# Right-hand blocks one per product, and factors, gates and block sums in idle PSUM banks

## The chip, the cores and the metric

The kernel runs on one core of one Trainium2 chip. The metric is device time in microseconds (us) from launch to end. The kernel before takes 1083.06 us, the median of three runs (1082.38 to 1083.61).

## The reference

Three parts follow one another on 4 batches of 448 rows, all in fp32: an attention with a sigmoid in place of the softmax (12 heads of 64), a gated layer, and a product layer.

```python
attn = 1 / (1 + exp(-(scale * q @ k.T - log(S))))      # S = 448
x    = (attn @ v) as 1792 x 768
xn   = x / sqrt(mean(x * x) + 1e-6) * rms_g
x    = (silu(xn @ w_gate) * (xn @ w_val)) @ w_out      # 768 -> 1536 -> 768
out  = ((x @ w1) * (x @ w2)) @ w3 @ w_out2             # 768 -> 1024 -> 1024 -> 768
```

## The kernel before

**Numbers.** The weights come as doubles. VectorE (DVE) turns them into fp32, and every fp32 operand of TensorE (PE) is split into a high and a low part: ScalarE (ACT) copies the high part (L134 for weights, L357 for activations), and the low part is the operand less the high part, on GpSimd (POOL, L137) for weights and on DVE (L362) for activations. A product runs three times (high by high, low by high, high by low), 448 columns at a time; all of them stand at L343. `w3 @ w_out2` is multiplied once, early, into `w3o`, so the last part has one matrix of 1024 x 768.

**Winograd's form.** For batches 2 and 3 of the gated layer, and for all four batches of the product layer and of the last matrix, a 2 x 2 block product is made with seven products in place of eight. This asks for block sums on three sides:

- sums of weight blocks (`winograd_blocks`, DVE L169, L170, L171, L177): `s1`, `s2` and `s2'` stand in a tile `s`, while the difference of a11 and a21 is written over a21 in the loaded tile `wd`. Each block is then split by ACT and POOL. In the first pass over the product layer the sums are also kept in DRAM for the second pass;
- sums of the right-hand operand (`right_blocks`): seven blocks w0 to w6, some of them factors such as b12 - b11, each split by ACT and DVE;
- sums of the seven products (`combine`, L617 to L637): each product ends in a PSUM bank, and DVE adds it to the sums before it (`u`, `v`, `c11`, `c21`).

**Order.** The stages that use this form are, one after the other: twelve gated tiles (`a_winograd`), the plain output of the gated layer, then for batches 0 and 1 eight product tiles (`c_winograd`, called c1 here) and three output steps (`d_winograd`, d1), and the same for batches 2 and 3 (c2, d2). A tile of `a_winograd` or `c_winograd` is seven products of nine matmuls. Two tiles of `c_winograd` make a pair: their four results `ab` are the four blocks from which the seven right-hand blocks of the output step are made, all in one piece after the pair's second tile. In `d_winograd` a product has two halves of six matmuls, and between the first halves and the second ones `y_blocks` makes seven right-hand blocks for the next pass from four tiles `ys` loaded out of DRAM.

**Queues.** Each engine works through its instructions in program order. A scheduler sorts them when the program is built, so the order of the lines is not quite that of the code.

**PSUM.** There are eight banks: three behind `psm()`, one of `ps_av`, and four behind `bank()`, which the seven products of a tile take in turn, so that a bank is needed again four products later. In c1 and c2 and in `a_winograd` the other four are not used. In `d_winograd` products 4 to 6 (of 0 to 6) stand in the three banks of `psm()`.

## Time and profile before

| | |
|---|---|
| median of three runs | 1083.06 us |
| the profiled execution | 1078.52 us |
| its span, first to last instruction | 1076.7 us |
| PE busy | 1055.8 us, 98% |
| DVE busy | 854.2 us, 79% |
| POOL busy | 507.8 us, 47% |
| ACT busy | 404.1 us, 38% |
| stage a_winograd | 508.7 to 664.3 us |
| stage c1 | 752.45 to 862.2 us |
| stage d1 | 862.2 to 918 us |
| stages c2 and d2 | 918 to 1026 us, 1026 to 1076.7 us |

The profile is of one execution, 4.54 us under the median. Of its 1078.52 us, 1.8 lie outside the span. Times of day in the rows count from the start of the span. In a row of a timeline the brackets hold the idle time of that engine just ahead of the row, and what ended it.

### The profile page before, as it was taken

Reading aid. Unit: us, or ns where it says so; the run is one execution under the profiler, and the core shown is the slowest. Engines: PE = TensorE matmul, PEld = TensorE weight load, DVE = VectorE, ACT = ScalarE, POOL = GpSimd, SP = SyncE. Lnnn points to the kernel's source line nnn. Section 1 sums busy time; section 2 is a strip of 40 time slices with the busy share of each in tenths; the row PEclk is TensorE's granted clock in tenths of the full one; section 3 lists DMA queues with packets and bytes.
Section 4 is the critical chain, followed back from the end, with each engine's and each line's share of the span. In section 5 each row is a group of like instructions: output and inputs, shape, how many; then the busy total and the mean of one; then the engine's idle time right before and its main releaser. Section 6 shows DMA issues by size and latency. Waiting matters only on the chain.

```text
span 1076.7 us, 14161 instructions
## 1 busy us (share of the span) xinstructions
PE 1055.8 (98%) x5080; PEld 884.6 (82%) x5080; DVE 854.2 (79%) x1132; ACT 404.1 (38%) x747; POOL 507.8 (47%) x414
## 2 busy tenths in 40 slices
PE   9999999999999999999999999999999989999998
PEld 4338799997766767699899998999988889999997
DVE  5998999999565787679787778676799899677874
ACT  5673311112243442215544444233333454333441
POOL 3646343543333232342655653233656666555572
PEclk9999999999999999999999999999999999999999
DMA  7743555566452567754311113766532245433221
GB/s 258 261 161 121 148 175 174 194 233 207 139 188 99 204 201 271 238 202 126 106 59 59 59 59 105 257 238 224 169 115 98 80 135 152 152 100 106 65 93 69
DMA packets 71350, 164.25 MB, mean 153 GB/s; under 512 B 7024, under 2 KB 45040, under 8 KB 71280
## 3 DMA queue, kind: packets, MB, share of 16 engines
q1 hardware_dynamic: 71280, 163.35, 45.5%
q8 instruction: 40, 0.66, 0.2%
q14 instruction: 30, 0.25, 0.1%
HBM read 119.67 MB, written 43.65 MB: 152 GB/s over the span
## 4 chain that ended last, share of the span: by engine, by line
PE 48%; DVE 7%; issue 2%; POOL 2%; DMA 2%; ACT 1%; SPq 0%; DVEq 0%; ACTq 0%; POOLq 0%
PE w L343 29%; PE psm L343 18%; POOL ws L137 2%; DVE w L362 1%; DMA wd<-in_wo 1%; DMA raw<-in_qkv 1%; DVE ab L655 1%; DVE s L177 0%; DMA wd<-in_w 0%; ACT ws L134 0%; PE av L454 0%; DVE wf L127 0%; DVE c L627 0%; DVE v L637 0%; DVE wf L116 0%
## 5 line engine op out<-in xcount | busy, mean ns | idle before, releaser
L343 PE MATMUL w<-w,ws 128*128 128x448 f32 x2052 | 424.4, 367 | 9.8 <-DVE v L625 9.0
L343 PEld LDWEIGHTS w<-w,ws 128*128 128x128 f32 x2052 | 385.7, 188 | 46.5 <-DVE v L625 11.8
L137 POOL TENSOR_TENSOR ws<-wf,ws 128x768 fp32r<-128x768 f32 (+1 forms) x92 | 175.4, 1911 | 112.3 <-ACT ws L134 95.0
L343 PE MATMUL psm<-hm,ws 128*128 128x448 f32 x864 | 178.0, 367 | 0.0
L343 PEld LDWEIGHTS psm<-hm,ws 128*128 128x128 f32 x864 | 161.9, 188 | 16.8 <-issue 2.4
L137 POOL TENSOR_TENSOR ws<-wd,ws 128x384 fp32r<-128x384 f32 (+1 forms) x128 | 131.3, 1040 | 75.9 <-ACT ws L134 74.3
L137 POOL TENSOR_TENSOR ws<-s,ws 128x384 fp32r<-128x384 f32 (+1 forms) x96 | 101.7, 1067 | 86.1 <-ACT ws L134 68.1
L136 POOL CAST ws<-wf 128x768 fp32r<-128x768 f32 (+1 forms) x52 | 46.4, 893 | 197.1 <-PE psm L343 98.4
L343 PE MATMUL psm<-x,ws 128*128 128x448 f32 x648 | 136.3, 368 | 0.2 <-DVE s L682 0.2
L343 PEld LDWEIGHTS psm<-x,ws 128*128 128x128 f32 x648 | 120.9, 188 | 17.0 <-issue 3.7
L116 DVE TENSOR_SCALAR wf<-mag 128x768 uint32<-128x768 uint32 (+1 forms) x76 | 67.0, 882 | 34.7 <-POOL ws L137 27.2
L124 DVE SCALAR_TENSOR_TENSOR wf<-wd,wf 128x768 uint32<-128x768 uint32 (+1 forms) x76 | 85.8, 1129 | 2.5
L114 DVE TENSOR_SCALAR mag<-wd 128x768 uint32<-128x768 uint32 (+1 forms) x76 | 52.0, 685 | 36.1 <-DMA wd<-in_wo 19.3
L127 DVE SCALAR_TENSOR_TENSOR wf<-wd,wf 128x768 uint32<-128x768 uint32 (+1 forms) x76 | 79.3, 1044 | 1.4
L134 ACT ACTIVATE ws<-wd 128x384 fp32r<-128x384 f32 (+1 forms) x128 | 57.2, 474 | 53.0 <-PE w L343 39.9
L343 PE MATMUL psm<-o,ws 128*128 128x384 f32 x384 | 70.4, 342 | 0.0
L343 PEld LDWEIGHTS psm<-o,ws 128*128 128x128 f32 x384 | 68.1, 190 | 2.7 <-issue 2.5
L115 DVE TENSOR_SCALAR mag<-mag 128x768 f32<-128x768 f32 (+1 forms) x76 | 64.2, 845 | 1.5
L134 ACT ACTIVATE ws<-s 128x384 fp32r<-128x384 f32 (+1 forms) x96 | 44.4, 475 | 49.4 <-DVE s L170 32.6
L454 PE MATMUL av<-a,raw 128*64 128x448 f32 x288 | 59.4, 548 | 0.0
L357 ACT ACTIVATE hm<-s 128x448 fp32r<-128x448 f32 x48 | 27.7, 576 | 71.3 <-DVE s L686 49.2
L169 DVE TENSOR_TENSOR s<-wd 128x384 f32<-128x384 f32 (+1 forms) x32 | 29.9, 934 | 30.6 <-POOL ws L137 28.7
(102 smaller groups left out, 1245.6 us busy)
## 6 DMA issues: line engine op xcount, KB each, us to landing
raw<-in_qkv SPq DMA_DIRECT2D x23, 736.0 KB, 5.1
wd<-in_wo SPq DMA_DIRECT2D x20, 768.0 KB, 5.6
wd<-in_w SPq DMA_DIRECT2D x16, 768.0 KB, 5.1
wd<-in_wg SPq DMA_DIRECT2D x12, 768.0 KB, 4.6
wd<-in_wv SPq DMA_DIRECT2D x12, 768.0 KB, 5.4
wd<-in_w SPq DMA_DIRECT2D x16, 512.0 KB, 4.3
w<-wf SPq DMA_DIRECT2D x16, 384.0 KB, 2.7
wd<-w SPq DMA_DIRECT2D x16, 384.0 KB, 3.7
```

What stands on the lines that cost most here:

```text
L114: nc.vector.tensor_scalar(out=mag.bitcast(U32), in0=hi, scalar1=0x7FFFFFFF, scalar2=None, op0=ALU.bitwise_and)
L115: nc.vector.tensor_scalar(out=mag, in0=mag, scalar1=HI_MIN, scalar2=HI_MAX, op0=ALU.max, op1=ALU.min)
L116: nc.vector.tensor_scalar(out=u, in0=mag.bitcast(U32), scalar1=3, scalar2=0x3FFFFFFF, op0=ALU.logical_shift_left, op1=ALU.bitwise_and,)
L124: nc.vector.scalar_tensor_tensor(out=u, in0=hi, scalar=0xC0000000, in1=u, op0=ALU.bitwise_and, op1=ALU.bitwise_or)
L127: nc.vector.scalar_tensor_tensor(out=u, in0=lo, scalar=29, in1=u, op0=ALU.logical_shift_right, op1=ALU.bitwise_or)
L134: nc.scalar.activation(t[:, 0, :w], f[:, :w], AF.Copy)
L136: nc.gpsimd.tensor_copy(out=t[:, 0, :w], in_=f[:, :w])
L137: nc.gpsimd.tensor_tensor(out=t[:, 1, :w], in0=f[:, :w], in1=t[:, 0, :w], op=ALU.subtract)
L169: nc.vector.tensor_tensor(out=s1, in0=a21, in1=a22, op=ALU.add)
L343: nc.tensor.matmul(ps, w, xt[:, xi, :], start=first and r == 0 and j == 0, stop=last and r == 2 and j == n - 1)
L357: i = nc.scalar.activation(dst[:, 0, :], src, AF.Copy)
L454: nc.tensor.matmul(av[p][d, :], r[:, v + j * D : v + (j + 1) * D], a[:, j, :], start=False, stop=(c == 2))
```

## The change

Three things are done.

First, the weight sum `s2'` is written over the block a12 in `wd` and no longer into `s`.

Second, the right-hand blocks come from a generator, `right_steps`, which gives one block at each `step()`; a step stands after every product in `combine` and after every first half in `d_winograd`. The low split of a block is issued one step later than its high split. The four results of a pair are used as they come, so three of the seven blocks of a pair are made before its second tile ends. In d1 the `ys` blocks are also spread over steps. Outside these stages (`x_blocks`, `y_blocks(0, k)`) the generator runs through at once.

Third, some DVE results go to PSUM: the factors t1 to t4 (`home`), `c11` and `c12` of gated and product tiles, the gate (silu in place, then times the value), and the fourth `ab` tile of each pair.

```diff
                 yield from (a11, s2, a12, a21, a22, s1)
-                nc.vector.tensor_tensor(out=s2, in0=a12, in1=s2, op=ALU.subtract)
+                nc.vector.tensor_tensor(out=a12, in0=a12, in1=s2, op=ALU.subtract)
                 if keep is not None:
-                    nc.sync.dma_start(out=keep[3], in_=s2)
+                    nc.sync.dma_start(out=keep[3], in_=a12)
...
-    def right_blocks(k, b11, b12, b21, b22, down=False):
+    def right_steps(k, b, home=None, down=False, wait=None):
+        def sub(out, in0, in1, op=ALU.subtract):
+            i = nc.vector.tensor_tensor(out=out, in0=in0, in1=in1, op=op)
+            if down or wait is not None:
+                tc.keep_in_program_order(i)
+        late = []
         def put(j, bl, src):
             t = acts["d" if down else "w", j, k] = ab_tile(f"w{j}", 7 * k + j) if down else right_tile(f"w{j}", bl)
-            split2(t, src)
+            nc.scalar.activation(t[:, 0, :], src, AF.Copy)
+            low()
+            late.append((t, src))
+        def low():
+            if late:
+                t, src = late.pop()
+                sub(t[:, 1, :], src, t[:, 0, :])
+        if wait is None:
+            put(0, 0, b[0])
+            yield
+            t1 = home()
+            sub(t1, b[1], b[0])
+            put(5, 1, t1)
+            yield
+            while len(b) < 4:
+                low()
+                yield
+            put(2, 0, b[2])
+            yield
+            t3 = home()
+            sub(t3, b[3], b[1])
+            put(3, 2, t3)
+            yield
+            t2 = home()
+            sub(t2, t3, b[0], ALU.add)
+            put(1, 2, t2)
+            yield
+            t4 = home()
+            sub(t4, b[2], t2)
+            put(4, 2, t4)
+            yield
+            put(6, 1, b[3])
+            yield
+            low()
+            return
...
+    def y_steps(k):
+        y = load_y(1, k)
+        for _ in range(2):
+            yield
+        yield from right_steps(k, y, wait=5 if k == 2 else 0)
+
+    def product_bank():
+        return psm()[:, :S]
...
-        combine(product, done)
+        combine(product, done, product_bank)
...
         for j in range(7):
             part(2 * n, j)
-        if between:
-            between()
+            step()
...
         p2 = product(2)
+        c11 = home() if home else scratch("c11")
         tt(out=c11, in0=p2, in1=u, op=ALU.add)
+        step()
...
         p3 = product(6)
-        tt(out=v, in0=p3, in1=v, op=ALU.add)
-        done(1, v, u)
+        c12 = home() if home else v
+        tt(out=c12, in0=p3, in1=v, op=ALU.add)
+        done(1, c12, u)
+        step()
...
-            s = scratch("s")
-            nc.scalar.activation(s, g, AF.Silu)
-            nc.vector.tensor_tensor(out=s, in0=s, in1=v, op=ALU.mult)
+            nc.scalar.activation(g, g, AF.Silu)
+            nc.vector.tensor_tensor(out=g, in0=g, in1=v, op=ALU.mult)
...
         def done(b, x, y):
-            t = ab[m % 2, b] = held("ab")
-            nc.vector.tensor_tensor(out=t, in0=x, in1=y, op=ALU.mult)
+            tiles.append(ps_av.tile([P, 512], F32, tag="av", bufs=1, name="ab")[:, :S] if len(tiles) == 3 else held("ab"))
+            nc.vector.tensor_tensor(out=tiles[-1], in0=x, in1=y, op=ALU.mult)
         winograd(first, m, done)
-        if m % 2:
-            right_blocks(m // 2, ab[0, 0], ab[0, 1], ab[1, 0], ab[1, 1], True)
+        if m % 2 == 0:
+            todo.append(right_steps(m // 2, tiles, product_bank, True))
...
     for m in range(KF2):
         c_winograd(i_c, m)
+    todo.extend(y_steps(k) for k in range(KD // 2))
     for n in range(KD // 2):
-        d_winograd(0, i_d, n, lambda: y_blocks(1, n))
+        d_winograd(0, i_d, n)
```

The counts of instructions of every engine stay as they were; what changes is where they stand and which tile they write. In the rows that follow, numbers behind a name tell instances apart, and the lines of the changed kernel are its own (L550 is `sub`, L699 the sum `v`, L703 `c11`, L718 `c12`, L738 the product tile, L178 `s2'`).

The first place is the end of a pair in c1, on DVE, in the kernel before:

```order
L655 TENSOR_TENSOR ab_6574<-v_6466,u_6465 128x448
L170 TENSOR_TENSOR s_6621<-s_6621,wd_6529 128x384
L556 TENSOR_TENSOR t1_6576<-ab_6574,t1_6576 128x448
L558 TENSOR_TENSOR ab_6463<-ab_6574,ab_6463 128x448
L560 TENSOR_TENSOR ab_6544<-ab_6544,t1_6576 128x448
L362 TENSOR_TENSOR w1_6588<-t1_6576,w1_6588 128x448
L362 TENSOR_TENSOR w3_6592<-ab_6463,w3_6592 128x448
L362 TENSOR_TENSOR w4_6596<-ab_6544,w4_6596 128x448
L362 TENSOR_TENSOR w6_6599<-ab_6574,w6_6599 128x448
L171 TENSOR_TENSOR wd_6529<-wd_6529 128x384
L625 TENSOR_TENSOR v_6603<-w_6631,u_6602 128x448
```

Seven operations on right-hand blocks stand in one piece (L556 to the last L362) ahead of the sum `v` of the next tile (L625). In the changed kernel the same place reads:

```order
L718 TENSOR_TENSOR psm_6588<-w_6578,v_6473 128x448
L738 TENSOR_TENSOR ab_6590<-psm_6588,u_6472 128x448
L550 TENSOR_TENSOR psm_6622<-ab_6590,ab_6470 128x448
L550 TENSOR_TENSOR w2_6592<-ab_6559,w2_6592 128x448
L699 TENSOR_TENSOR v_6595<-w_6627,u_6594 128x448
L550 TENSOR_TENSOR psm_6638<-psm_6622,ab_6437 128x448
L550 TENSOR_TENSOR w3_6624<-psm_6622,w3_6624 128x448
L178 TENSOR_TENSOR wd_6544<-wd_6544,s_6612 128x384
L703 TENSOR_TENSOR psm_6658<-w_6643,u_6594 128x448
L550 TENSOR_TENSOR psm_6660<-ab_6559,psm_6638 128x448
L550 TENSOR_TENSOR w1_6640<-psm_6638,w1_6640 128x448
```

Ahead of `v` (L699) stand now the product tile, one factor and one low split; the other factors follow between the sums of the next tile, and those named psm are in PSUM.

The second place is the start of d1 on PE: the first half of product 4 of its first step (three runs of two matmuls, psm_7388) and the start of product 5, with what each instruction waits for. Before:

```order
L343 MATMUL psm_7388<-w4_6596,ws_7297 128x448 [waits Activation_49]
L343 MATMUL psm_7388<-w4_6853,ws_7297 128x448
L343 MATMUL psm_7388<-w4_6596,ws_7297 128x448 [waits Pool_49]
L343 MATMUL psm_7388<-w4_6853,ws_7297 128x448
L343 MATMUL psm_7388<-w4_6596,ws_7297 128x448
L343 MATMUL psm_7388<-w4_6853,ws_7297 128x448
L343 MATMUL psm_7389<-w5_6581,ws_7297 128x448 [waits Activation_49]
```

Products 4 and 5 wait for ACT, which makes the high part of a block. In the changed kernel, where psm_7395 and psm_7396 are these products:

```order
L344 MATMUL psm_7395<-w4_6662,ws_7327 128x448 [waits DVE_49,Activation_49]
L344 MATMUL psm_7395<-w4_6924,ws_7327 128x448
L344 MATMUL psm_7395<-w4_6662,ws_7327 128x448 [waits Pool_49]
L344 MATMUL psm_7395<-w4_6924,ws_7327 128x448
L344 MATMUL psm_7395<-w4_6662,ws_7327 128x448
L344 MATMUL psm_7395<-w4_6924,ws_7327 128x448
L344 MATMUL w_7391<-w0_7010,ws_7358 128x448 [waits Activation_49]
L344 MATMUL psm_7396<-w5_6513,ws_7327 128x448 [waits DVE_49]
```

Product 4 now waits for DVE too and product 5 for DVE, and one matmul of product 0's bank (w_7391) has moved ahead of product 5. The rows of DVE at the end of the last pair, before:

```order
L362 TENSOR_TENSOR w2_7366<-ab_7316,w2_7366 128x448 [waits Activation_49]
L655 TENSOR_TENSOR ab_7356<-v_7237,u_7236 128x448 [waits DVE_49]
L177 TENSOR_TENSOR s_7332<-wd_7272,s_7332 128x256 [waits Pool_49]
L556 TENSOR_TENSOR t1_7358<-ab_7356,t1_7358 128x448 [waits DVE_49]
L558 TENSOR_TENSOR ab_7234<-ab_7356,ab_7234 128x448
L560 TENSOR_TENSOR ab_7316<-ab_7316,t1_7358 128x448 [waits DVE_49]
L362 TENSOR_TENSOR w1_7370<-t1_7358,w1_7370 128x448 [waits Activation_49]
L362 TENSOR_TENSOR w3_7374<-ab_7234,w3_7374 128x448 [waits Activation_49]
L362 TENSOR_TENSOR w4_7378<-ab_7316,w4_7378 128x448 [waits Activation_49]
L362 TENSOR_TENSOR w6_7381<-ab_7356,w6_7381 128x448
L169 TENSOR_TENSOR s_7428<-wd_7340 128x256 [waits DMAHW4_49,Pool_49]
```

and in the changed kernel:

```order
L718 TENSOR_TENSOR psm_7385<-w_7375,v_7259 128x448 [waits DVE_49,PE_49]
L178 TENSOR_TENSOR wd_7295<-wd_7295,s_7362 128x256 [waits Pool_49]
L738 TENSOR_TENSOR ab_7387<-psm_7385,u_7258 128x448 [waits DVE_49]
L550 TENSOR_TENSOR psm_7411<-ab_7387,ab_7256 128x448 [waits DVE_49]
L550 TENSOR_TENSOR w2_7389<-ab_7346,w2_7389 128x448
L550 TENSOR_TENSOR psm_7422<-psm_7411,ab_7222 128x448 [waits Activation_49]
L550 TENSOR_TENSOR w3_7413<-psm_7411,w3_7413 128x448
L170 TENSOR_TENSOR s_7450<-wd_7370 128x256 [waits DMAHW5_49,Pool_49]
L550 TENSOR_TENSOR psm_7433<-ab_7346,psm_7422 128x448 [waits Activation_49]
L550 TENSOR_TENSOR w1_7424<-psm_7422,w1_7424 128x448
```

The tiles psm_7411, psm_7422 and psm_7433 are t3, t2 and t4 of the last pair. They stand in the three banks that products 4 to 6 of d1 take, and each bank is free for its product when the low split of its factor (w3_7413, w1_7424, and w4_7435 three rows on) has read it. The sums t2 and t4 also wait for ACT, which copies the high part out of the tile that they read.

The third place is on DVE in the first step of d1, around the sum `v`. Before:

```order
L177 TENSOR_TENSOR s_7428<-wd_7340,s_7428 128x256
L362 TENSOR_TENSOR w5_7475<-t1_7470,w5_7475 128x448
L362 TENSOR_TENSOR w2_7478<-ys_7466,w2_7478 128x448
L556 TENSOR_TENSOR t1_7470<-ys_7468,t1_7470 128x448
L558 TENSOR_TENSOR ys_7464<-ys_7468,ys_7464 128x448
L560 TENSOR_TENSOR ys_7466<-ys_7466,t1_7470 128x448
L362 TENSOR_TENSOR w1_7482<-t1_7470,w1_7482 128x448
L362 TENSOR_TENSOR w3_7486<-ys_7464,w3_7486 128x448
L362 TENSOR_TENSOR w4_7490<-ys_7466,w4_7490 128x448
L362 TENSOR_TENSOR w6_7493<-ys_7468,w6_7493 128x448
L625 TENSOR_TENSOR v_7497<-w_7385,u_7496 128x448
```

All of the blocks made from `ys` stand ahead of `v` (L625). In the changed kernel:

```order
L550 TENSOR_TENSOR w4_7435<-psm_7433,w4_7435 128x448
L550 TENSOR_TENSOR w6_7459<-ab_7387,w6_7459 128x448
L178 TENSOR_TENSOR wd_7370<-wd_7370,s_7450 128x256
L550 TENSOR_TENSOR t1_7506<-ys_7477,ys_7475 128x448
L550 TENSOR_TENSOR t2_7508<-ys_7481,t1_7506 128x448
L699 TENSOR_TENSOR v_7497<-w_7392,u_7496 128x448
L550 TENSOR_TENSOR ys_7477<-ys_7481,ys_7477 128x448
L550 TENSOR_TENSOR w1_7510<-t2_7508,w1_7510 128x448
L703 TENSOR_TENSOR c11_7540<-w_7393,u_7496 128x448
```

Two factors stand ahead of `v` (L699), and the splits follow it one by one.

## Rows read from the trace of the kernel before

**Rows 1.** The page, busy time, share of the span and instructions of PE and DVE.
```profile
PE 1055.8 (98%) x5080; PEld 884.6 (82%) x5080; DVE 854.2 (79%) x1132; ACT 404.1 (38%) x747; POOL 507.8 (47%) x414
```

**Rows 2.** Waits of PE: total us, times, longest us.
```profile
PE w L343 <- DVE v L625: 9.0, 4, 2.9
...
PE w L343 <- DVE c L627: 0.8, 2, 0.6
```

**Rows 3.** Timeline of PE, 508 to 918: start, us, tile, count, idle before and releaser.
```profile
520.59 141.50 PE L343 MATMUL w<-w,ws 128*128 128x448 f32 x693 [0.55 <-DVE c L627]
...
752.45 35.03 PE L343 MATMUL w<-w,ws 128*128 128x448 f32 x171
789.23 26.04 PE L343 MATMUL w<-w,ws 128*128 128x448 f32 x126 [1.75 <-DVE v L625]
817.57 25.98 PE L343 MATMUL w<-w,ws 128*128 128x448 f32 x126 [2.31 <-DVE v L625]
845.59 21.68 PE L343 MATMUL w<-w,ws 128*128 128x448 f32 x105 [2.04 <-DVE v L625]
867.10 3.85 PE L343 MATMUL psm<-w,ws 128*128 128x448 f32 x18
...
883.61 5.48 PE L343 MATMUL w<-w,ws 128*128 128x448 f32 x18 [2.93 <-DVE v L625]
888.93 3.83 PE L343 MATMUL psm<-w,ws 128*128 128x448 f32 x18
```

**Rows 4.** Timeline of DVE at the end of a pair in c1.
```profile
782.72 0.61 DVE L556 TENSOR_TENSOR t<-ab,t 128x448 f32<-128x448 f32 x1
...
784.86 3.32 DVE L362 TENSOR_TENSOR w<-ab,w 128x448 fp32r<-128x448 f32 x3
...
788.57 0.61 DVE L625 TENSOR_TENSOR v<-w,u 128x448 f32<-128x448 f32 x1
```

**Rows 5.** Timeline of DVE in the first step of d1.
```profile
876.17 0.95 DVE L177 TENSOR_TENSOR s<-wd,s 128x256 f32<-128x256 f32 x1 [0.64 <-POOL ws L137]
...
880.80 2.22 DVE L362 TENSOR_TENSOR w<-ys,w 128x448 fp32r<-128x448 f32 x3
882.94 0.61 DVE L625 TENSOR_TENSOR v<-w,u 128x448 f32<-128x448 f32 x1
```

**Rows 6.** Windows: length, busy us of each engine, granted clock, DMA share, GB/s.
```profile
752.45:862.20 109.75, 103.66 (x505) 94.37 (x504) 93.79 (x137) 43.08 (x91) 67.63 (x61) 1.00 0.35 117
862.20:918.00 55.80, 52.87 (x252) 48.29 (x252) 52.70 (x85) 27.67 (x65) 34.68 (x36) 0.97 0.45 136
918.00:1026.00 108.00, 108.00 (x529) 98.62 (x528) 82.40 (x119) 41.24 (x69) 59.63 (x39) 1.00 0.34 105
...
886.00:888.00 2.00, 2.00 (x7) 1.73 (x7) 2.00 (x5) 1.03 (x3) 1.98 (x3) 0.50 0.45 167
```

**Rows 7.** DVE groups in c1 by shape: busy us, mean ns, idle before.
```profile
L362 DVE TENSOR_TENSOR w<-ab,w 128x448 fp32r<-128x448 f32 x16 | 16.2, 1044 | 0.0
L655 DVE TENSOR_TENSOR ab<-c,c 128x448 f32<-128x448 f32 x8 | 8.0, 996 | 0.1
...
L169 DVE TENSOR_TENSOR s<-wd 128x384 f32<-128x384 f32 x7 | 7.1, 1017 | 8.5 <-POOL ws L137 8.5
...
L625 DVE TENSOR_TENSOR v<-w,u 128x448 f32<-128x448 f32 x8 | 4.9, 612 | 0.0
```

**Rows 8.** Line L655 in c1: ns least, median, most.
```profile
L655 DVE TENSOR_TENSOR ab<-v,u x7: 610/614/1442, 768.4 to 854.7; 128x448 f32<-128x448 f32 x7
```

**Rows 9.** Timeline of ACT at the end of c1.
```profile
858.73 0.42 ACT L134 ACTIVATE ws<-s 128x256 fp32r<-128x256 f32 x1 [1.90 <-PE w L343]
...
860.54 0.58 ACT L357 ACTIVATE w<-t 128x448 fp32r<-128x448 f32 x1 [1.08 <-PE w L343]
```

**Rows 10.** Timeline of POOL near the end of c2.
```profile
1018.63 0.74 POOL L137 TENSOR_TENSOR ws<-s,ws 128x256 fp32r<-128x256 f32 x1 [1.38 <-ACT ws L134]
```

**Rows 11.** Timeline of DVE at the start of a_winograd.
```profile
518.64 1.35 DVE L177 TENSOR_TENSOR s<-wd,s 128x384 f32<-128x384 f32 x1 [0.76 <-POOL ws L137]
```

More of the change, by code (lines that the diff above doesn't have):

```diff
@@ L541, in ab_tile @@
         return right_tile(name, (n - 2 * KF1) // 2)
[L543 to L545 removed]
+    def right_steps(k, b, home=None, down=False, wait=None):
[4 more added lines that the diff above has]
+        late = []
         def put(j, bl, src):
             t = acts["d" if down else "w", j, k] = ab_tile(f"w{j}", 7 * k + j) if down else right_tile(f"w{j}", bl)
[L549 to L562 removed]
+            nc.scalar.activation(t[:, 0, :], src, AF.Copy)
[33 more added lines that the diff above has]
+            return
+        t1 = scratch("t1")
+        sub(t1, b[1], b[0])
+        t2 = scratch("t2")
+        sub(t2, b[3], t1)
+        put(1, 2, t2)
+        yield
+        sub(b[1], b[3], b[1])
+        put(3, 2, b[1])
+        yield
+        sub(t2, b[2], t2)
+        put(4, 2, t2)
+        yield
+        for _ in range(wait):
+            low()
+            yield
+        for j, bl, x in ((0, 0, b[0]), (2, 0, b[2]), (5, 1, t1), (6, 1, b[3])):
+            put(j, bl, x)
+            yield
+        low()
@@ L564, in x_blocks, with load_y @@
     def x_blocks(k):
-        right_blocks(k, load_x(2, k), load_x(3, k), load_x(2, k + 3), load_x(3, k + 3))
+        for _ in right_steps(k, [load_x(b, m) for m in (k, k + 3) for b in (2, 3)], bank):
+            pass
     yd = {}
-    def y_blocks(g, k):
+    def load_y(g, k):
         y = []
@@ L574, in y_blocks, with step @@
                 nc.sync.dma_start(out=y[-1], in_=yd.pop((g, b, m)))
-        right_blocks(k, *y)
+        return y
+    def y_blocks(g, k):
+        for _ in right_steps(k, load_y(g, k), bank):
+            pass
+    todo = []
+    def step():
+        if todo:
+            next(todo[0], None)
+            if inspect.getgeneratorstate(todo[0]) == inspect.GEN_CLOSED:
+                todo.pop(0)
+    def y_steps(k):
+        y = load_y(1, k)
+        for _ in range(2):
+            yield
+        yield from right_steps(k, y, wait=5 if k == 2 else 0)
+    def product_bank():
+        return psm()[:, :S]
     def bank():
@@ L589, in product, with d_winograd @@
             return ps
-        combine(product, done)
-    def d_winograd(g, first, n, between=None):
+        combine(product, done, product_bank)
+    def d_winograd(g, first, n):
         ps = [bank() if j < 4 else psm()[:, :S] for j in range(7)]
@@ L632, in combine @@
         done(0, c11, c21)
+        step()
         p5 = product(5)
@@ L840, in fused_kernel @@
         c_winograd(i_c, m)
+    todo.extend(y_steps(k) for k in range(KD // 2))
     for n in range(KD // 2):
-        d_winograd(0, i_d, n, lambda: y_blocks(1, n))
+        d_winograd(0, i_d, n)
+    assert not todo
     for m in range(KF2):
@@ L846, in fused_kernel @@
         d_winograd(1, i_d2, n)
+    assert not todo
     pools["xw"].release()
```

28 lines of the change are left out of this document (12 added, 16 removed).

## The prediction, made before the changed kernel ran

> **What bounds the kernel now.** I read the busy times first. PE is busy for 98% of the span and DVE for 79% [rows 1], so work taken from DVE counts only where PE stands still for it. Next come the waits of PE: in the stages that the change touches, PE waits six times for DVE, 9.0 us for the sum `v` and 0.8 us for `c` [rows 2]. The timeline of PE puts them in place: 1.75, 2.31 and 2.04 us in c1, each after a pair of tiles, 2.93 us inside d1, and 0.55 us at the start of a_winograd (the other `c` wait, 0.8 less 0.55, is at its end) [rows 3]. Between these PE runs without a break; 693 matmuls in 141.50 us give 0.2042 us each [rows 3], so a product of nine in c1 takes 1.84 us, a pair of tiles (126 matmuls) 25.7 us, a half product of six in d1 1.225 us.
>
> The timeline of DVE says why `v` is late. At the end of a pair the block operations run from 782.72, `v` starts only at 788.57, and PE goes on at 789.23 [rows 3, 4]. In d1 it is the same: splits of `ys` blocks up to 882.94, then `v`, then PE at 883.61 [rows 3, 5].
>
> The wait in d1 costs more than 2.93 us. [...] The 18 matmuls from 883.61 to 888.93 take 5.32 us where 18 x 0.2042 = 3.68 would do [rows 3]: 1.64 us more. The three waits of c1, up to 2.31 us long, have no such stretch: the window over all of c1 shows 1.00 [rows 6].
>
> **The change part by part.** No instruction is added on any engine; some are moved, some write another memory.
>
> *Right-hand blocks one per product, c1.* Before, seven block operations stand between a pair's last product tile and the next `v`. Now one factor and one low split do. A bank of a product is needed again four products later, so `v` has three products, 5.5 us, from the end of its own. What can stand ahead of it: a product tile (1.44 at most [rows 8]), a factor (0.61 [rows 4]), a low split (1.04 [rows 7]) and a weight sum held by POOL, on average 8.5/7 = 1.2 us and then 1.02 [rows 7]. That is 5.3 us if all meet at their worst, 3.9 with the product tile and the split at 0.61. So `v` should be in time and the three waits go: -(1.75 + 2.31 + 2.04) = -6.10 us. I take all of it; the bounds are 0 (the weight sum in front becomes the new wait) and 6.10.
>
> What is late next is DVE's own load. In c1 it is busy for 93.8 of 109.75 us [rows 6]. Reading from PSUM costs no more than reading SBUF here: `v`, with one operand in PSUM, takes 612 ns [rows 7], L556 with both in SBUF 0.61 us [rows 4]. The forms with two SBUF operands spread further, to 996 ns for `ab` from two `c` tiles and 1044 ns for the low splits of `ab` [rows 7]. With `c11` in PSUM the first fall to 612: 8.0 - 8 x 0.612 = 3.1 us. Three of five of those splits now read PSUM: 16.2 x 3/5 - 9.6 x 0.612 = 3.8 us. That leaves 93.8 - 6.9 = 86.9 us, 21.7 a pair beside 25.7 on PE. Writing to PSUM by DVE has no row. I take 0.61 us, since the side of the operand made no difference in reading; the bounds are 0.61 and 1.44, the dearest such operation with both operands in SBUF [rows 8]. Where it is dearer is the third rival.
>
> *`ys` blocks spread, d1.* The splits no longer stand ahead of `v`, only two sums do. `v` can run some 11 to 12 us after the start of d1, and PE needs its bank after fifteen half products, 18.4 us. The 2.93 us go, and with them the slow stretch: -4.57 us. Bounds: 0 and -4.57. DVE is full there (52.7 of 55.8 us [rows 6]), but what slides goes into c2, where it has 25.6 of 108 us free [rows 6]. The loads of `ys` wait for tiles that the last pair still holds, and the queue of SP waits with them; `v` does not depend on them.
>
> *New waits at the start of d1 and d2.* Products 4, 5 and 6 of the first step stand in the three PSUM banks that now hold t3, t2 and t4 of the last pair, and their blocks are made only after c1's last product. With T0 as the end of that product (867.10 less 24 matmuls, 862.2 [rows 3]), PE comes to product 4 at T0 + 4 x 1.225 = 4.90. Until then DVE must do, in this order: the weight sum `s2'`, which waits for ACT's high copy of a12 (0.42 [rows 9], from 0.08) and POOL's low part (0.74 [rows 10]), so it starts at 1.38; 0.95 for itself less 0.08 of overlap [rows 5], so the product tile starts at 2.25; t3 from 2.93 (0.61 and 0.06 between dependent ones); ACT copies t3 from 3.6 to 4.18 (0.58 [rows 9]); t2 runs from 4.24 to 4.86, and the low split of t3 from 4.77 to 5.39. The bank is free at 5.46: a wait of 0.56 us. The next bank holds t2. Its low split stands behind a weight sum and t4 and ends at 7.32, released 7.39, while PE, now 0.56 late, comes at 6.89 (matmul ahead of it counted): 0.50 us. Product 6 then finds t4's bank free. That is 1.06 us, and the same once more at d2: +2.1 us. The bounds are 0 (POOL earlier by 0.6) and 2.0 each (`s2'` held by 1 us more), so 0 to 4.0. These waits are shorter than the 2.31 us after which the clock stayed up, so I add no slow stretch.
>
> Why t2 waits for ACT is in the order, not in a row: both read the bank of t3. [...]
>
> *`s2'` over a12.* The tile `s` is free earlier, by one ACT and one POOL step, so the first sum of the next weights waits less; `wd` is free later by the same, and the next load has the time of a tile (63 matmuls, 12.9 us) to hide that. In exchange `s2'` must wait for POOL to have read a12. At the start of a_winograd it waited already, 0.76 us before 518.64, and ended right ahead of the `c` that PE waited for [rows 3, 11]. I leave the 0.8 us of `c` waits as they are: 0, bounds -0.8 and +0.8.
>
> *Gates and `c` in PSUM, a_winograd; c2.* PE waits nowhere inside the 141.50 us of a_winograd [rows 3] or in c2, busy for all of 108.0 us [rows 6]: 0, covered by PE.
>
> **Sum**, against the profiled run: 1078.52 - 6.10 - 4.57 + 2.1 = 1069.95 us. The median of the runs is 4.54 higher; the same difference gives 1083.06 - 8.57, about 1074.5 us.
>
> **The rivals.**
> *The waits in c1 stay.* The weight sums stand in program order among the block operations, and one held by POOL (1.2 us on average [rows 7]) holds `v` too. For it: 5.3 against 5.5 us is near. Against it: all must be at their worst at once, three times. If c1 gains nothing: -4.57 + 2.1 = -2.5, 1080.6 us.
>
> *No new waits.* If POOL and the first sums run 0.6 us sooner, both starts of d cost nothing and `c` at a_winograd may go as well: -6.10 - 4.57 - 0.8 = -11.5, 1071.6 us. Against it: the chain at T0 is one of dependent steps.
>
> *Slower: DVE's writes to PSUM are dear.* A pair has nine of them (four `c`, four t, one `ab`). At a price of 0.61 + x DVE needs 21.7 + 1.3 (two holds of 0.64 [rows 5]) + 9x a pair and passes PE's 25.7 at x = 0.3. At 1.2 us (x = 0.59) it is 28.3, 2.6 x 4 = 10.4 us over PE, in place of 6.1 of waits: +4.3. The chain at a start of d has four such writes in line (`c12`, t3, t2, t4), +2.4 each: 2 x (1.06 + 2.4) = +6.9. With -4.57 that is +6.6, about 1089.7 us; at 1.44 us some 1100. It decides against the change from about 1.05 us an operation. For it: no row has such a write, and nine a pair is many. Against it: reads of PSUM sit at 612 ns, more evenly than SBUF ones.
>
> *The change does not move the waits.* The rows of the order show one factor and one split ahead of `v` where seven operations stood, so this would need DVE to be late as a whole, with 21.7 beside 25.7 us: 1083.1.
>
> **How the numbers follow.** Forecast 0.60, its own range 1071.6 (no new waits) to 1076.4 (waits of 2.0 at both starts). Waits in c1 stay wholly or in part: 0.18, 1076.4 to 1081.2. Dear writes: 0.12. No effect: 0.05. The rest, 0.05, lies below 1071.6. The range to hold 8 in 10 is 1071.0 to 1081.2: it takes in the first two and, below, 0.6 us, half the spread of the three runs; left out are the dear writes, no effect and a little below. A measurement tells 0.2%, 2.2 us, from no change: faster than 1080.9 has 0.60 + 0.16 + 0.05 = 0.81, same 0.02 + 0.05 + 0.01 = 0.08, slower 0.11.
>
> **What would show it.** Right, if PE's waits for `v` in c1 and in the middle of d1 are gone and the clock around the second step of d1 is 1.00; if new waits of 0.3 to 2 us stand before the `psm` matmuls at the start of d1 and d2, released by DVE's low splits; if DVE's operations writing PSUM take about 0.61 us. Wrong, if PE waits for `v` or `c` each pair behind a weight sum, if a DVE write to PSUM takes over 0.9 us, or if the waits at the starts of d exceed 2 us each and bring a stretch of low clock with them.

## The result

The changed kernel takes 1070.57 us (median of four runs, 1069.37 to 1073.0) beside 1083.34 us for the kernel before on the same chip (1082.38 to 1085.12): a ratio of 0.9886, interval 0.9863 to 0.9909. It is faster, as forecast, by 12.8 us where 8.6 were forecast, and its median lies 0.4 us below the range of 1071.0 to 1081.2. On two other chips the same kernel was compared again: 1071.99 beside 1081.38 (0.9918, 0.9896 to 0.9940) and 1072.39 beside 1082.22 us (0.9914, 0.9889 to 0.9939), a gain of 9.4 and 9.8 us. So the size of the gain itself differs by some 3 us between comparisons; the three intervals overlap.

The profiled execution of the changed kernel takes 1069.8 us, its span is 1067.8. Against the profiled run of before that is 8.7 us less, nearly the 8.57 of the sum. The rest of the 12.8 us, 4.1, is in what lies between a profiled run and a median (4.8 us before, 0.8 in the changed kernel), and that is where the forecast went wrong.

### The profile page after: what moved, and what is told of

Same layout as the page of the kernel before. It is cut to its first block, busy times and chain, and to the rows that moved or that the text cites. A ratio compares the mean times of both kernels' runs of the same rounds, so it can differ in the third digit from the quotient of the medians.

```text
span 1067.8 us, 14132 instructions
## 1 busy us (share of the span) xinstructions
PE 1052.4 (99%) x5080; PEld 882.1 (83%) x5080; DVE 831.6 (78%) x1132; ACT 400.4 (37%) x747; POOL 490.0 (46%) x414
## 5 line engine op out<-in xcount | busy, mean ns | idle before, releaser
L138 POOL TENSOR_TENSOR ws<-wf,ws 128x768 fp32r<-128x768 f32 (+1 forms) x92 | 172.8, 1880 | 105.2 <-ACT ws L135 95.7
L138 POOL TENSOR_TENSOR ws<-wd,ws 128x384 fp32r<-128x384 f32 (+1 forms) x160 | 155.3, 986 | 127.5 <-ACT ws L135 102.7
L135 ACT ACTIVATE ws<-wd 128x384 fp32r<-128x384 f32 (+1 forms) x160 | 70.7, 476 | 60.9 <-PE w L344 42.3
L125 DVE SCALAR_TENSOR_TENSOR wf<-wd,wf 128x768 uint32<-128x768 uint32 (+1 forms) x76 | 90.1, 1186 | 2.3
L138 POOL TENSOR_TENSOR ws<-s,ws 128x384 fp32r<-128x384 f32 (+1 forms) x64 | 62.1, 971 | 51.0 <-ACT ws L135 47.7
L128 DVE SCALAR_TENSOR_TENSOR wf<-wd,wf 128x768 uint32<-128x768 uint32 (+1 forms) x76 | 77.6, 1021 | 1.3
L116 DVE TENSOR_SCALAR mag<-mag 128x768 f32<-128x768 f32 (+1 forms) x76 | 61.9, 815 | 1.3
L135 ACT ACTIVATE ws<-wf 128x768 fp32r<-128x768 f32 x40 | 33.8, 846 | 54.5 <-DMA wf<-wo 22.4
L178 DVE TENSOR_TENSOR wd<-wd,s 128x384 f32<-128x384 f32 (+1 forms) x32 | 26.9, 841 | 34.8 <-POOL ws L138 34.8
L344 PE MATMUL psm<-w,ws 128*128 128x448 f32 x216 | 47.1, 369 | 2.9 <-ACT w L558 2.4
```

Of the source, the lines that this page charges most:

```text
L116: nc.vector.tensor_scalar(out=mag, in0=mag, scalar1=HI_MIN, scalar2=HI_MAX, op0=ALU.max, op1=ALU.min)
L125: nc.vector.scalar_tensor_tensor(out=u, in0=hi, scalar=0xC0000000, in1=u, op0=ALU.bitwise_and, op1=ALU.bitwise_or)
L128: nc.vector.scalar_tensor_tensor(out=u, in0=lo, scalar=29, in1=u, op0=ALU.logical_shift_right, op1=ALU.bitwise_or)
L135: nc.scalar.activation(t[:, 0, :w], f[:, :w], AF.Copy)
L138: nc.gpsimd.tensor_tensor(out=t[:, 1, :w], in0=f[:, :w], in1=t[:, 0, :w], op=ALU.subtract)
L178: nc.vector.tensor_tensor(out=a12, in0=a12, in1=s2, op=ALU.subtract)
```

## The profile after

The busy times of the page, against [rows 1]: PE is at 99%.

```profile
PE 1052.4 (99%) x5080; PEld 882.1 (83%) x5080; DVE 831.6 (78%) x1132; ACT 400.4 (37%) x747; POOL 490.0 (46%) x414
```

The waits of PE (total, times, longest), against [rows 2]: `v` and `c` of c1 and of a_winograd are gone, and new waits stand in their place.

```profile
PE psm L344 <- ACT w L558: 2.4, 2, 1.9
...
PE w L344 <- DVE v L714: 0.8, 1, 0.8
...
PE psm L344 <- DVE c L709: 0.2, 1, 0.2
```

The timeline of PE, against [rows 3] (start, length, tile, count, idle time before):

```profile
507.54 154.44 PE L344 MATMUL w<-w,ws 128*128 128x448 f32 x756
...
749.99 105.48 PE L344 MATMUL w<-w,ws 128*128 128x448 f32 x516
856.29 2.69 PE L344 MATMUL w<-w,ws 128*128 128x448 f32 x12 [0.81 <-DVE v L714]
860.85 1.46 PE L344 MATMUL psm<-w,ws 128*128 128x448 f32 x6 [1.87 <-ACT w L558]
...
1017.04 1.46 PE L344 MATMUL psm<-w,ws 128*128 128x448 f32 x6 [0.57 <-ACT w L558]
```

a_winograd and c1 run without a break. At the start of d1 there are two waits, 0.81 us for `v` of c1's last tile and 1.87 us ahead of product 4, and at the start of d2 one of 0.57 us.

The windows of c1 and d1 (length, busy times, clock), against [rows 6]:

```profile
749.99:852.91 102.92, 102.92 (x506) 94.58 (x505) 85.93 (x136) 41.63 (x90) 59.75 (x59) 1.00 0.37 118
852.91:908.71 55.80, 52.76 (x253) 46.64 (x252) 51.56 (x81) 27.59 (x65) 35.03 (x36) 1.00 0.46 137
```

c1 takes 102.92 us for 109.75, DVE in it 85.93 for 93.79 us. d1 takes 55.80 us. In the kernel before it takes 56.07 us up to PE's first matmul of c2 at 918.27; the window of [rows 6] ends 0.27 us ahead of that. So the wait in its middle and the low clock are gone, and the waits at its start have taken nearly the same time. By stages of the two profiles: up to a_winograd -1.15 us (508.69 to 507.54, not touched), a_winograd -1.31 (155.58 to 154.27), c1 -6.83, d1 -0.27, c2 and d2 +0.66. That c1 gives 6.83 and not 6.10 is in the waits themselves: 504 matmuls at 0.2042 us are 102.92, so each of these waits cost about 0.24 us more than the idle time that its row shows.

The 1.15 us in front are not the change's. In the attention PE waits for `w3ot` (2.58 us before, 2.40 us in the changed kernel), and behind this wait the clock falls in the profile of before and not in that of the changed kernel. The windows of before, then of the changed kernel:

```profile
118.00:120.00 2.00, 2.00 (x5) 1.22 (x4) 2.00 (x2) 1.09 (x2) 1.54 (x1) 0.50 1.02 232
```

```profile
118.00:120.00 2.00, 2.00 (x12) 1.92 (x11) 2.00 (x2) 1.03 (x2) 1.91 (x1) 1.00 1.00 242
```

Of two later profiles of the changed kernel one has a mean clock of 1.0 and comes to a_winograd at 508.22 us. The other has 0.998, no fall from 480 to 1034 us, and comes there at 510.79.

DVE's groups in c1 (busy us, mean ns), against [rows 7]:

```profile
L550 DVE TENSOR_TENSOR w<-psm,w 128x448 fp32r<-128x448 f32 x12 | 7.4, 614 | 0.0
...
L738 DVE TENSOR_TENSOR ab<-psm,c 128x448 f32<-128x448 f32 x7 | 4.4, 624 | 0.2
...
L718 DVE TENSOR_TENSOR psm<-w,v 128x448 f32<-128x448 f32 x7 | 4.3, 620 | 0.0
```

The write to PSUM, for which no row stood before, takes 620 ns. The product tile falls from 996 to 624 ns and the low splits that now read PSUM from 1044 to 614. Among the product tiles of before the long ones are those that run beside POOL: of 15 in c1 the ten that run while POOL is idle take 0.61 to 0.63 us, the five beside an instruction of POOL 1.16 to 1.44 us. Three rows of before, then two of the changed kernel, where a product tile beside POOL stays at 0.62 us:

```profile
768.43 1.44 DVE L655 TENSOR_TENSOR ab<-v,u 128x448 f32<-128x448 f32 x1
...
768.36 1.02 POOL L137 TENSOR_TENSOR ws<-wd,ws 128x384 fp32r<-128x384 f32 x1 [1.44 <-ACT ws L134]
769.36 1.39 POOL L137 TENSOR_TENSOR ws<-s,ws 128x384 fp32r<-128x384 f32 x1
```

```profile
787.00 0.62 DVE L738 TENSOR_TENSOR ab<-psm,c 128x448 f32<-128x448 f32 x1
...
786.34 2.00 POOL L138 TENSOR_TENSOR ws<-wd,ws 128x384 fp32r<-128x384 f32 x2 [3.16 <-ACT ws L135]
```

## The experiments

Two readings of the 4 us that the forecast missed stood against each other. T1: a wait costs in every execution what the profiled one shows. T2: the clock falls after such waits in some executions and places and not in others, and the profiled run of before had few falls. Below, the time lost to the clock is an estimate: the mean over the executions of time multiplied by one less the mean granted clock, so that an execution with 0.993 has lost 7.5 us. For the fall in d1 of before the same working gives 1.70 us (0.72, 0.50 and 0.93 in the three windows of 2 us from 884 to 890), and the 18 matmuls there took 1.64 us more.

**The kernel before once more.** No edit.

> The kernel before, unchanged, to see its single executions with span and mean granted clock. Theory T1 (the waits cost in every execution what the profiled one shows, and the 4.5 us between profile and median are of another kind, which the change keeps): the slow executions show a mean clock of 0.997 like the profiled one, and PE waits of 9.0 us for v. Theory T2 (the clock falls after the waits for v, but in a different number of places in each execution; the profiled one had a single fall): executions of 1082 to 1085 us show a mean clock of about 0.992 to 0.994, that is 3 to 5 us of time at the lower level, and a profile among them shows the low clock after the waits in c1 too.

Measured: 12 executions from 1078.71 to 1086.89 us. The shortest shows a mean clock of 0.997, the longest 0.989; over 35 executions on this chip the time goes along with the clock, and the mean loss is 7.1 us. The profiled run of 1078.52 us, at 0.997, lost 3.2 us, in two falls: the one of d1 and the one at 118 us that is shown above. The new profile (span 1081.3, clock 0.992) has waits of the same kind. Its timeline of PE, then three of its windows:

```profile
790.55 27.57 PE L343 MATMUL w<-w,ws 128*128 128x448 f32 x126 [1.76 <-DVE v L625]
819.89 27.50 PE L343 MATMUL w<-w,ws 128*128 128x448 f32 x126 [1.78 <-DVE v L625]
849.15 21.66 PE L343 MATMUL w<-w,ws 128*128 128x448 f32 x105 [1.75 <-DVE v L625]
887.15 6.62 PE L343 MATMUL w<-w,ws 128*128 128x448 f32 x18 [2.93 <-DVE v L625]
```

```profile
792.00:794.00 2.00, 2.00 (x7) 1.75 (x7) 1.86 (x4) 0.00 (x0) 1.02 (x1) 0.50 0.31 107
822.00:824.00 2.00, 2.00 (x6) 1.75 (x6) 1.86 (x5) 0.54 (x2) 0.36 (x1) 0.50 0.47 126
888.00:890.00 2.00, 2.00 (x7) 1.74 (x7) 2.00 (x6) 1.02 (x3) 1.19 (x2) 0.50 0.58 209
```

After 1.76 and 1.78 us in c1 the clock goes to 0.50, and the 126 matmuls behind take 27.5 us and not the 26.04 of [rows 3]; after 1.75 us it does not. So behind a wait of this length the low clock came in one place or execution and not in the next. T2 holds, T1 falls.

**Three waits added to the changed kernel.**

```diff
-        tt(out=v, in0=p6, in1=u, op=ALU.add)
+        for _ in range(1 + again):                  # 12 for m = 1, 3, 5 of c2
+            tt(out=v, in0=p6, in1=u, op=ALU.add)
```

> The changed kernel with the sum v of three tiles of c2 (the second, fourth and sixth) computed thirteen times in a row instead of once, with the same result, so that PE waits about 2 us at each of three places where it had no wait. T1 (a wait costs its own length): slower by the sum of the three waits in the profile, about 5 to 7 us, and a mean clock as in the changed kernel. T2 (each wait of this size also brings, in most executions, a stretch at the lower clock, about 1.4 us each as in the kernel before): 4 us on top, about 10 us slower than the changed kernel, and a mean clock of about 0.994 to 0.995.

Measured: 1087.6 us, 17 us over the changed kernel's first median, mean clock 0.9931. The waits came out longer than meant, 3.16 to 3.19 us. Timeline of PE in c2, and windows behind the first, second and third wait:

```profile
937.29 2.52 PE L344 MATMUL w<-w,ws 128*128 128x448 f32 x9 [3.16 <-DVE v L700]
940.46 26.45 PE L344 MATMUL w<-w,ws 128*128 128x448 f32 x117 [0.65 <-DVE psm L704]
970.10 28.77 PE L344 MATMUL w<-w,ws 128*128 128x448 f32 x126 [3.19 <-DVE v L700]
1002.05 34.27 PE L344 MATMUL w<-w,ws 128*128 128x448 f32 x167 [3.19 <-DVE v L700]
```

```profile
940.00:942.00 2.00, 1.54 (x4) 1.42 (x5) 1.91 (x4) 0.00 (x0) 0.00 (x0) 0.50 0.56 182
972.00:974.00 2.00, 2.00 (x7) 1.76 (x7) 1.51 (x4) 0.00 (x0) 0.00 (x0) 0.50 0.07 23
1004.00:1006.00 2.00, 2.00 (x11) 1.86 (x10) 1.86 (x5) 0.00 (x0) 0.00 (x0) 1.00 0.02 5
```

Behind two of three equal waits the clock goes to 0.50, behind the third it stays at 1.00. The executions lose 7.5 us to the clock where the changed kernel loses 2 to 3, so, as an estimate across chips, 1.5 to 1.8 us for each wait on top of its length, as T2 says and in a stage that had shown neither.

**Only the `ys` blocks spread.** The generator for `ys` put into the kernel before.

```diff
         for j in range(7):
             part(2 * n, j)
-        if between:
-            between()
+            step()
```

> Of the change only the spreading of the ys blocks over the steps of d1; weight sums, the lump after each pair and the memories are as before. T1: -4.6 us against before (2.93 us of wait and 1.64 us of slow matmuls), 1078.5. T2: the same wait is gone, with whatever falls of the clock came after it, but those after the waits in c1 stay: between -3 and -6 us. A rival (the wait moves): the sums of the next weights are late in its place, and less than 2 us are gained.

Measured: 1086.94 us, ratio 1.0048 (1.0033 to 1.0063): slower. The wait moved, as the rival said, and grew. Waits of PE, then DVE's timeline between `v` and `c`:

```profile
PE w L344 <- DVE c L683: 5.4, 4, 3.6
...
PE psm L344 <- DVE c L689: 1.6, 1, 1.6
```

```profile
880.63 0.62 DVE L680 TENSOR_TENSOR v<-w,u 128x448 f32<-128x448 f32 x1
...
882.78 2.23 DVE L597 TENSOR_TENSOR w<-t,w 128x448 fp32r<-128x448 f32 x2
884.93 2.21 DVE L597 TENSOR_TENSOR w<-ys,w 128x448 fp32r<-128x448 f32 x2
887.06 0.61 DVE L683 TENSOR_TENSOR c<-w,u 128x448 f32<-128x448 f32 x1
```

The splits that stood ahead of `v` now stand between `v` and `c`, at 1.1 us each. Moving them gains nothing here, where DVE is busy for 48.5 of the 50 us from 864 to 914.

**The `ys` blocks in one piece in the changed kernel.**

```diff
         for j in range(7):
             part(2 * n, j)
             step()
+        if between:
+            between()                                # the old right_blocks(n, *load_y(1, n))
```

> The changed kernel with the ys blocks of d1 made in one piece again, between the first halves and the second ones, with their factors in SBUF. T1: 4.6 us slower than the changed kernel, about 1075. T2: slower by the wait in d1 (about 2.9 us) and by a fall of the clock in part of the executions, 3 to 5 us, about 1074 to 1075.5, with a mean clock under that of the changed kernel. If DVE has slack in d1 now, the wait is shorter than 2.9 us and less is lost.

Measured: 1072.33 us, 0.9907 (0.9891 to 0.9924). Its profile has no wait of 2.9 us in d1, and the stages are those of the changed kernel (from product 4 of d1 on 48.01 us beside 47.86). So the wait inside d1 went without the spreading. Two things differ there from the kernel before: PE comes to this place later, by the waits of 0.83 and 1.86 us at the start of d1, and `v` starts 18.6 us after the start of d1 where it was 20.7, since four of the block operations stand behind it and not ahead of it. What happens without the waits at the start is told below, with the starts of d1 and d2.

**Steps without PSUM.**

```diff
-        combine(product, done, product_bank)
+        combine(product, done)
-            todo.append(right_steps(m // 2, tiles, product_bank, True))
+            todo.append(right_steps(m // 2, tiles, lambda: scratch("t"), True))
```

The fourth ab tile and the gate are back in SBUF too.

> The changed kernel with every factor, c11, c12, gate and ab tile in SBUF, as in the kernel before; the steps and the s2' over a12 stay. Theory S (the order does it: one block per product lets v through): the waits in c1 are gone all the same and the time is within 2 us of the changed kernel, about 1071 to 1073. Theory M (the memory does it: DVE is only in time because operations with an operand in PSUM stay at 0.61 us beside POOL): DVE needs some 7 us more in c1 and more in d1, waits of 1 to 3 us per pair come back, and the time is 1076 or more.

Measured: 1078.47 us, 0.9963 (0.9951 to 0.9976). The three waits of about 2 us in c1 have become nine of 0.24 to 0.94 us, 4.5 us in all. The two longest, of 0.94 us each, are for weights: PE waits for ACT's copy. One of these, one for `v`, and the splits of factors in c1:

```profile
799.46 13.13 PE L344 MATMUL w<-w,ws 128*128 128x448 f32 x63 [0.94 <-ACT ws L135]
812.92 5.72 PE L344 MATMUL w<-w,ws 128*128 128x448 f32 x27 [0.34 <-DVE v L718]
```

```profile
L550 DVE TENSOR_TENSOR w<-t,w 128x448 fp32r<-128x448 f32 x12 | 9.9, 821 | 0.0
```

Theory M holds: the order alone leaves DVE too slow (821 ns where PSUM gives 614). That it gains 4.6 us all the same is the clock: 2.3 us are lost where before on that chip lost 7.7, and in its profile, with a mean clock of 0.997, the clock is 1.00 in every window from 480 to 1034 us, behind the short waits of c1 too.

**PSUM without steps.**

```diff
-        if m % 2 == 0:
-            todo.append(right_steps(m // 2, tiles, product_bank, True))
+        if m % 2:
+            for _ in right_steps(m // 2, ab.pop(m // 2), product_bank, True):
+                pass
```

The `ys` blocks are in one piece as well.

> The changed kernel with the seven right-hand blocks of a pair issued in one piece after its second tile, and the ys blocks in one piece too; factors, c11, c12, gates and the fourth ab stay in PSUM. Theory S: the waits for v in c1 come back in part, since the scheduler may still sort within the piece: 1.0 to 2 us each in c1, with clock falls, 1076 to 1080. Theory M: the shorter operations are enough; within 2 us of the kernel with only the ys blocks in one piece, about 1072 to 1073.

Measured: 1070.42 us, 0.9882 (0.9861 to 0.9903), the whole gain. c1 has no wait:

```profile
750.77 109.56 PE L344 MATMUL w<-w,ws 128*128 128x448 f32 x535
```

Theory S falls: with the memory, the steps are not needed. One reservation: the piece is not closed. Of the eleven DVE operations on a pair's blocks the scheduler puts five between the last product tile and `v` and six behind `v`, where the kernel before has seven ahead of it. That the memory alone would do in the very order of before is not shown.

**`s2'` alone, and `c11`, `c12` and the gates alone.** The first is the change's `winograd_blocks` in the kernel before, the second this:

```diff
-        combine(product, done)
+        combine(product, done, lambda: psm()[:, :S])   # factors, ab and weight sums as before
```

> Of the change only the weight sum s2' written over a12. Both theories of the waits: it touches no wait for v; the first sums of the next weights start earlier. Within 1.5 us of before, 1081.5. If the weight sums were what holds DVE at the end of a pair, it would be 3 us or more faster.

> Of the change only c11, c12 and the gates in PSUM; the factors, the ab tiles, the pieces after each pair and inside d1 and the weight sums are as before. Theory M, with the sums c as the main part: the product tiles fall from 996 and 731 to about 620 ns, 2 us a pair, nearly the length of a wait in c1, and half or more of the waits of c1 goes: -4 to -8 us. If the factors' splits (16.2 us in c1 at 1044 ns) are the main part: waits of 1 to 1.5 us stay after each pair and in d1, and the gain is under 3 us.

Measured: `s2'` 1082.6 us, 1.0002 (0.9983 to 1.002), nothing that can be measured. The sums `c` 1076.45 us, 0.9963 (0.9946 to 0.9979): 4.9 us, half of the 9.4 that the changed kernel gains on the same chip, and within the 4 to 8 expected. The mechanism was not as expected: waits of 1.36, 1.77 and 1.75 us stay in c1, 4.88 us for 6.10, a fifth less and not half, and 1.86 stay in d1. Most of the gain is clock, a mean loss of 3.2 us for 6.6. So the factors and the ab tile bring the rest of the waits. Those were not run by themselves.

**The starts of d1 and d2.** The factors of the last pair in SBUF, run twice, the second time beside the changed kernel; and two forms of it with the `ys` blocks, or all blocks, in one piece.

```diff
-            todo.append(right_steps(m // 2, tiles, product_bank, True))
+            home = product_bank if m < KF2 - 2 else lambda: scratch("t")
+            todo.append(right_steps(m // 2, tiles, home, True))
```

> The changed kernel with the factors t2, t3 and t4 of the last pair of c1 and of c2 in SBUF, so that products 4 to 6 of d1 and d2 find their PSUM banks free. If the bank waits are what the profile shows at the start of d1 and d2 (1.87 and 0.57 us, and 0.81 us for v ahead of it), the first two go: -2.4 us against the changed kernel, about 1068. Rival: DVE is late there in any case, and the wait moves to the matmuls of the second halves: within 0.7 us of the changed kernel.

> The changed kernel with the factors of the last pairs in SBUF once more, now on the chip of the changed kernel. By the stages of the profiles (from c1 on 314.3 against 317.8 us) it is 3 us faster; if the waits of the changed kernel at the starts of d also cost clock, its mean clock is higher by 0.001 or more and the medians differ by 4 us or more.

> The kernel with both lumps and PSUM homes, with the factors of the last pair of c1 and c2 in SBUF. If the waits at the starts of d1 and d2 are for the banks of those factors, the 1.24 and 1.22 us that the profile of the lump kernel shows there go: about 1068, 2.4 us under that kernel. Rival: they are for ACT's copies of the late blocks, which the bank does not change: 1070.

> The changed kernel with the factors of the last pairs in SBUF and the ys blocks in one piece. The spreading of ys is worth nothing by the run that had it alone and by the run that left it out: within 1 us of the kernel with the factors of the last pairs in SBUF (0.9875 of before), and the wait of 1.56 us in d1 that this one had is shorter. Rival: with d1 starting 2.7 us earlier the piece stands in the way of v again: a wait of 2 to 3 us in d1, 1070 to 1072.

Measured: 1068.67 (0.9875, 0.9858 to 0.9893) and 1069.84 us (0.9889, 0.9866 to 0.9912; the changed kernel beside it 1072.39); the forms in one piece 1070.86 and 1070.18 beside 1071.99. The waits at both starts are gone, in all four runs, so those of 1.87 and 0.57 us were for the banks. The one of 0.81 us for `v` went with them, which was not expected. In the first run one of 1.56 us for `v` comes later in d1, where DVE is busy for 48.3 of the 50 us from 864 to 914:

```profile
890.75 3.96 PE L344 MATMUL w<-w,ws 128*128 128x448 f32 x18 [1.56 <-DVE v L699]
```

With 1.1 to 2.6 us against the changed kernel on the same chips all three forms are on the better side of it, though their intervals overlap with its own; the first has the shortest time of all kernels run. Beside the changed kernel it shows no better clock (0.9977 and 0.998), so the expected 4 us were not there: the waits at the starts of d cost no clock that these runs can tell.

The two forms in one piece missed what was expected of them. With all blocks in one piece the ratio is 0.9909, where that kernel without this edit had 0.9882 on another chip: no gain, and waits of 1.34 and 0.75 us stand in d1. With the `ys` blocks in one piece a part of the old wait is back, at the place of the 2.93 us of before:

```profile
879.09 3.95 PE L344 MATMUL w<-w,ws 128*128 128x448 f32 x18 [1.65 <-DVE v L722]
```

So the piece is in the way of `v` again as soon as PE is not held at the start of d1: the rival, with 1.65 us for its 2 to 3. Spread, the wait of 1.56 us comes a little later instead, so by these runs neither form is the better one.

**One block moved.** For the last pair, w2 is made after w6.

```diff
-            put(2, 0, b[2])
+            if not last:
+                put(2, 0, b[2])
             yield
             t3 = home()
```

> The changed kernel with one block moved: for the last pair w2 is made after w6, not ahead of t3, so that ACT's copy of w5 does not stand behind that of w2, which waits for the product tile. If the held split of w5 is what makes DVE late at the starts of d1 and d2, the wait for v at the start of d1 (0.81 us) goes and the one for the bank shrinks by 0.5 us or more at both places: 1.3 to 2.3 us less wait in the profile. Rival (DVE is late by its own load there, and the banks decide): the waits stay within 0.4 us of 0.81, 1.87 and 0.57.

Measured: 1073.49 us, 0.9917 (0.9892 to 0.9941), beside 1072.39 for the changed kernel: no gain. Its PE rows at d1 and d2:

```profile
858.82 2.69 PE L344 MATMUL w<-w,ws 128*128 128x448 f32 x12 [0.17 <-DVE v L719]
862.86 1.46 PE L344 MATMUL psm<-w,ws 128*128 128x448 f32 x6 [1.35 <-ACT w L558]
...
1020.36 1.45 PE L344 MATMUL psm<-w,ws 128*128 128x448 f32 x6 [0.55 <-ACT w L558]
```

At d1 the waits shrink by 1.2 us as the theory asks, at d2 they do not, and small waits later in d1, 0.9 us where the changed kernel has 0.24, take part of it back. So the held split is a part of the term, at d1 alone; the banks are the larger one.

**The changed kernel on two more chips.** No edit.

> The changed kernel, unchanged, with more executions and on the same chip as the next three, to see how much of its gain is clock. T2: against before about -12 us, of which about 6 are clock (before loses some 7 us a run to the lower level, span times one less the mean clock, the changed kernel 1 to 2) and 6 are waits; the executions of both, each multiplied by its mean clock, differ by only 5 to 7 us. T1: the clock of both is alike and the whole difference is in the product.

> The changed kernel on the same chip as the two above. Against before 0.988 to 0.992, as in its two earlier comparisons (0.9886 and 0.9918); mean clock 0.997 to 0.999.

| chip | kernel | executions | median us | mean clock | lost to the clock | mean time less that |
|---|---|---|---|---|---|---|
| second | before | 17 | 1081.38 | 0.9939 | 6.6 | 1074.5 |
| second | changed | 6 | 1071.99 | 0.9972 | 3.0 | 1068.8 |
| third | before | 11 | 1082.22 | 0.9935 | 7.0 | 1075.2 |
| third | changed | 6 | 1072.39 | 0.9980 | 2.2 | 1070.3 |

By the unrounded figures the gain parts into 3.5 to 4.8 us of clock and 4.9 to 5.8 us of the rest; less clock than the 6 expected, more than the sum had.

## Why the prediction came out as it did

**The failed step is the clock term, and with it the step from the profiled run to the median.** The forecast put the clock at 1.64 us, for one wait, behind which [rows 6] have 0.50 from 886 to 888, and said of the three waits of c1 that they have no such stretch. That was read from one execution, with a clock of 0.997 and near the lower end of all executions of that kernel. In others the same waits do bring it, and the mean loss of before is 6.6 to 7.7 us. For the same reason "the same difference" may not be taken off the median: the 4.54 us between profile and median were in part clock that the change takes away too. (The executions of before in the first comparison have no clock on record; this is read from the 35 later ones.) With the measured 3.5 to 4.8 us in place of 1.64 the sum gives 10.4 to 11.7 us, between the measured 9.4 and 12.8.

**The waits of c1, -6.10 us: right in size, laid to the wrong part of the change.** They are gone, with 6.83 us. But by the two experiments on steps and PSUM it is the memory more than the place of the operations: steps without PSUM leave 4.5 us of waits, PSUM without steps none, in an order that the scheduler had eased. The forecast had the fall of the operations to 0.61 us in its working, 6.9 us of DVE time in c1; it used it only to show that DVE had room. One figure there is off and nothing rests on it: with the product tile and the split at 0.61 us, what can stand ahead of `v` adds up to 4.05 us, not 3.9. The rows show what the memory did: with both operands in SBUF the product tile took 1.16 to 1.44 us beside POOL, with one in PSUM 0.62 us; on average the product tiles and the low splits went from 996 and 1044 ns to 624 and 614.

**The wait in d1, -4.57 us: gone, and not by the spreading alone.** Spread alone it cost 5 us; left out of the changed kernel it changed nothing, but there the waits at the start held PE back, and without them 1.65 us of the wait returned. d1 as a stage gained 0.27 us, since what went in its middle came back at its start.

**The waits at the starts of d, +2.1 us: found in the right place, 1.1 us too small.** 0.81 + 1.87 and 0.57 us are 3.25, so d1 cost 1.6 us more than its 1.06 and d2 0.5 us less. The working of that chain starts with `s2'` and has no place for the sums that DVE still owes ahead of `c12`, as if `c12` could start 0.08 us after T0. DVE's rows in the changed kernel, then ACT's (T0 is 852.91):

```profile
853.82 0.61 DVE L713 TENSOR_TENSOR u<-w,u 128x448 f32<-128x448 f32 x1
854.99 0.62 DVE L550 TENSOR_TENSOR w<-psm,w 128x448 fp32r<-128x448 f32 x1 [0.55 <-ACT w L558]
855.53 0.61 DVE L714 TENSOR_TENSOR v<-w,v 128x448 f32<-128x448 f32 x1
856.25 0.63 DVE L718 TENSOR_TENSOR psm<-w,v 128x448 f32<-128x448 f32 x1
...
858.30 0.63 DVE L550 TENSOR_TENSOR psm<-ab 128x448 f32<-128x448 f32 x1
...
860.09 0.61 DVE L550 TENSOR_TENSOR w<-psm,w 128x448 fp32r<-128x448 f32 x1
```

```profile
853.94 0.58 ACT L558 ACTIVATE w<-ab 128x448 fp32r<-128x448 f32 x1 [1.64 <-DVE ab L738]
854.43 0.53 ACT L558 ACTIVATE w<-psm 128x448 fp32r<-128x448 f32 x1
```

`c12` starts at 856.25, 3.3 us after T0. DVE was behind, and the low split of w5 held it for 0.55 us more, because ACT copies w2, which waits for its product tile, ahead of w5. The order had shown `c12` ahead of `s2'`; what DVE had left at T0 was not reckoned. From `c12` on the chain ran as worked out: t3 2.05 us behind it (2.85 forecast, with `s2'` no longer in the way of POOL), the split that frees the bank 1.8 us behind t3 (1.84). That t2 waits for ACT's copy of t3, as the chain has it, is in two profiles: here the copy ends at 859.51 and t2 starts at 859.54, and with one block moved DVE stands idle for 0.61 us ahead of t2, released by ACT's L558. The row of PE names ACT and not DVE as the last, since ACT's copy of t2 ends at 860.75 and DVE's split at 860.70; that it is the bank is shown by the runs with the factors in SBUF.

**The `c` waits, 0 with bounds of 0.8: at the lower bound.** Both are gone. `s2'` over a12 did not do it by itself, since alone it leaves one of 0.89 us there; which part did, no run shows. **DVE's writes to PSUM: right**, 0.62 us for 0.61, so the rival on the slower side had no part. **The sum against the profiled run**, -8.57 for -8.7, agrees by luck: d1 gave 3.2 us less than the 3.51 put down for it, and 2.5 us from a_winograd and from the stages ahead of it made up for that. The 1.15 of these that lie ahead of it go with the fall of the clock in the attention, which one of the two profiles happened to have.

What stays open: what decides whether the clock falls after a given wait (of three waits of 3.16 to 3.19 us in one execution two had a fall behind them), why the first comparison shows 3 us more gain than the two later ones, and the shares of the factors and the fourth ab tile.

## What to carry over

Before a profile's waits are priced, look at the mean clock of several executions: where it lies under 1 (0.993 to 0.994 for the kernel before), a wait can have cost more than its length, as the one of 1.76 us in c1 did (27.57 us for the 126 matmuls behind it, for 26.04), and a profile that happens to be a quick execution (0.997) hides that. Here results in idle PSUM banks were worth more than the better order (a ratio of 0.9882 without the steps, 0.9963 without PSUM): the operations themselves became shorter, the product tile from 996 to 624 ns. And check at the joints of stages who held the new tile's bank last, and what stands ahead of that instruction on every engine.
